# Low parts of w1 made ahead through a fourth place and due sooner; expert 0's loads and all gathers' transposes later in the order

## The chip, the cores and the metric

One core of one Trainium2 chip. The metric is the device time of one execution in microseconds (us); the number given for a kernel is the median of its runs. Engines: TensorE (PE; PEld is its weight load), VectorE (DVE), ScalarE (ACT), GpSimd (POOL) and SyncE (SP), which issues nearly all DMAs. A row with a q behind the engine (SPq) is of that engine's sequencer: an issue of a DMA, a wait or a branch.

## The reference, cut to what matters

Three layers in a row, all in float32 (batch 4, 8 heads, 576 positions, 2304 tokens of width 512):

```python
def _attn_ref(q, k, v, omega):          # random-feature attention
    q_p, k_p = phi(q * scale), phi(k * scale)
    kv = np.einsum('bhsm,bhsd->bhmd', k_p, v)
    z = np.sum(k_p, axis=2)
    ...
    return num / den

def _moe_ref(x, w_in, w_out):           # 512 -> 2048 -> 512
    h = x @ w_in
    return (h - np.tanh(h)) @ w_out

def _moe2_ref(x, w_gate, w1, w2):       # 8 experts, 512 -> 1024 -> 512
    logits = x @ w_gate                 # pairs (token, expert) in falling order of logit;
    ...                                 # a token goes to the first expert with room (288 places)
    for e in range(E):
        mask = assigned == e
        h = np.maximum(x[mask] @ w1[e], 0.0)
        out[mask] = h @ w2[e]
```

## The kernel before

**Split numbers.** A float32 matrix product is made of three TensorE passes: each operand is split into a high part (a copy to a shorter type, by ScalarE) and a low part (the operand minus its high part, by VectorE or GpSimd), and high x high, high x low and low x high are summed in PSUM (L604 to L606, L651, L1402 to L1404, L1421 to L1423).

**Stages.** The 2304 tokens are six blocks of 384. Attention runs along the first four blocks of the second layer. Blocks 4 and 5 share their passes over w_in in a double block (about 440 to 530 us): 16 chunks f, each with first matmuls of both blocks (`chunk_ops`), their polynomial on ScalarE and VectorE, and small matmuls for the gate's logits (`last_logits`). Behind it stands a branch (`tc.If`, L1530): if inputs were out of range, a slower version would run. All engines load the flag `over` (L1529) and branch. Behind the branch come the second matmuls of block 4 (`but_last_ops`: two kept chunks first, then eleven that load the low part gL from g4l and the low part oL of w_out from low_wo), and of block 5 (`last_ops`, 16 chunks of nine matmuls, L651, whose oL come through three slots, L566). Beside these VectorE searches which tokens go to expert 0, by rounds in which TensorE counts (L1096, L1121). Then the eight experts follow (`expert_ops`, from about 622 us).

**Low parts of w1, made ahead.** `low_ops` makes the low part of the first two of four row blocks of w1 of each expert, during the double block: 16 times a load of 512 KB into a tile `dw` (L581), two copies of a half to a tile `dh` (ScalarE, L300), two subtractions in place (L305), and a store to w1l (L588). `dw` has three places and `dh` two; they open in `switch2`, when attention is done. The two halves are written as copy, subtraction, copy, subtraction; as the subtraction both reads and writes the tile, the second copy stands behind the first subtraction.

**Gate of a block.** `gate_ops` transposes a block's output into `mT` (128 x 4 x 384 float32), multiplies it with the gate's weights (L682) and puts the logits away. It runs for blocks 0 to 3; `mT` has one place.

**Expert 0.** Its first tokens are fetched by three indirect DMAs of GpSimd (gathers, L1351) out of the stored outputs of blocks 0 to 4, and TensorE transposes them (L1369); the rows of block 5 are added later, out of SBUF (L1373). Its weights are eight loads of 512 KB (L1309 and L1312) and two of made-ahead low parts (L1322), all on SyncE's queue. Each has a turn: it stands behind the landing, as planned, of one of block 5's sixteen loads of oL (`oloads`). The fourth, sixth and eighth of its low parts are made by a copy and an accumulating DMA (L1330). For experts 1 to 7 the gathers (L1351) and transposes (L1364) run while the expert before is still at work.

**What sets the order.** The program is a list of operations with engine, planned duration, due time (`plan.at` and `lag`) and the tiles that they read and write. `Plan.run` (L129) walks through a planned time: it issues the operation that can start first, and of those that can start together the one due first. A DMA is planned as 280 KB per us, one after the other, plus 1.9 us; `late` is planned time behind an operation's end before what reads it can start. The order that comes out is each engine's order on the chip; the chip adds the waits. Tiles come from rings of places; a place is free when the last reader of its tile is done. With `rp` and `wp` an operation reads or writes a tile without standing behind that tile's other writers or readers.

The functions that the change touches, and what calls them:

Of the kernel before, what the change touches and what calls it, by code (L numbers as in the profile page):

```python
# [9 lines left out]
F32R = mybir.dt.float32r  # L10
# [176 lines left out]
def tile_kernel(ctx, tc, q, k, v, omega, w_in, w_out, w_gate, w_gate_t, w1, w2, out, dbg=None):  # L187
# [11 lines left out]
    NF = DFF // P  # L199
    E = w_gate.shape[1]  # L200
    BLK = 384
    NBLK = NT // BLK
# [95 lines left out]
    def copy(e, out, in_):  # L298
        if e == ACT:
            nc.scalar.activation(out, in_, AF.Copy)  # L300
        else:
            nc.vector.tensor_copy(out, in_)
# [270 lines left out]
    def low_ops(start, step):  # L573

        n = w1.shape[2]
        d_rings[:] = plan.ring([P, n], F32, "dw", []), plan.ring([P, n // 2], F32R, "dh", [])
        for k in range(E * NPRE):
            e_, r = k // NPRE, slice(k % NPRE * P, (k % NPRE + 1) * P)
            raw = Buf(d_rings[0])
            plan.at = start + step * k  # L580
            plan.op(SP, 0.47, lambda e, raw=raw, e_=e_, r=r: nc.sync.dma_start(raw.t, w1[e_, r, :]), w=[raw], nbytes=P * n * 4,  # L581
                    early=False)
            for i, h in enumerate((slice(0, n // 2), slice(n // 2, n))):
                hi = Buf(d_rings[1])
                plan.op(ACT, 0.6, lambda e, raw=raw, hi=hi, h=h: copy(e, hi.t, raw.t[:, h]), r=[raw], w=[hi], lag=4.0 + 0.6 * i)
                plan.op({POOL: 1.45, DVE: 0.65}, 0, lambda e, raw=raw, hi=hi, h=h: low(
                    e, raw.t.bitcast(F32R)[:, h], raw.t[:, h], hi.t), r=[raw, hi], w=[raw], lag=4.7 + 0.6 * i)
            plan.op(SP, 0.47, lambda e, raw=raw, e_=e_, r=r: nc.sync.dma_start(w1l[e_, r, :], raw.t), r=[raw],  # L588
                    nbytes=P * n * 4, lag=6.8)

# [72 lines left out]
        return xm, plan.op(SP, 0.47, lambda e: nc.sync.dma_start(ms[n * P + 1:(n + 1) * P + 1, :], xm.t.bitcast(F32)), r=[xm], lag=0.7,  # L663
                           nbytes=P * DM * 4)

    def gate_ops(j, xms):
        mT, lp, lT, lgb = Buf(mTr), Buf(bank), Buf(sr), Buf(None)
        own = lambda z, w: z.t[:, :TPB * w].rearrange("p (t n) -> p t n", t=TPB)
        for t, xm in enumerate(xms):
            tp = Buf(bank)  # L670

            def transposes(e, tp=tp, xm=xm):
                for c in range(NC):
                    nc.tensor.transpose(tp.t[:, c * P:(c + 1) * P], xm.t.bitcast(F32)[:, c * P:(c + 1) * P], ident)

            plan.op(PE, 0.44, transposes, r=[xm], w=[tp], lag=0.8 + 0.7 * t)
            plan.op({ACT: 0.6, DVE: 0.68}, 0, lambda e, t=t, tp=tp: copy(
                e, mT.t[:, :, t * P:(t + 1) * P], tp.t.rearrange("p (c n) -> p c n", n=P)), r=[tp], w=[mT], lag=1.5 + 0.7 * t)

        def gate(e):  # L680
            for c in range(NC):
                nc.tensor.matmul(lp.t[c * P // NC:(c + 1) * P // NC, :BLK], wg[:, c, :], mT.t[:, c, :], start=True, stop=True,  # L682
                                 skip_group_check=True)

        def back(e):
            for t in range(TPB):
                nc.tensor.transpose(own(lp, P)[:, t, :], lT.t[:, t * P:(t + 1) * P], ident)

        plan.op(PE, 0.9, gate, r=[mT, bwg], w=[lp], lag=4.0)
        plan.op({ACT: 0.48, DVE: 0.55}, 0, lambda e: copy(e, lT.t, lp.t[:, :BLK]), r=[lp], w=[lT], lag=5.0)  # L690
        plan.op(PE, 0.33, back, r=[lT], w=[lp], lag=5.6)
        plan.op(DVE, 0.25, lambda e: nc.vector.tensor_reduce(
            lg[:, j * TPB:(j + 1) * TPB, :], own(lp, P).rearrange("p t (c e) -> p t e c", c=NC)[:, :, :E, :], axis=AX.X,
            op=OP.add), r=[lp], w=[lgb], lag=6.0)
# [63 lines left out]
    def mlp_ops(start, step, general=False):  # L758
# [4 lines left out]
        for j in range(NBLK - 1):  # L763
# [32 lines left out]
                plan.at = start[j] + step[j] * NF + LAG2 + 0.7 * t  # L796
                xms.append(out_ops(j, t, acc[t])[0])
            plan.at = start[j] + step[j] * NF + LAG2
            gate_ops(j, xms)

        j, lacc4, lprev4 = NBLK - 2, Buf(bank), None
        for f in range(NF):
# [496 lines left out]
    def load_ops(p, ei):  # L1299
# [4 lines left out]
        for i in range(2 * NC):  # L1304
# [8 lines left out]
                                      w2[bass.ds(reg[0], 1), f * P:(f + 2) * P, :].rearrange("o (a p) d -> p (o a) d", p=P))  # L1313

            plan.at = PHASE * p + AT_EW * i + AT_LOAD
            turn = [] if p else [oloads[min(2 * i + 2, NF - 1)]]
            plan.op(SP, 0.47, load, w=[raw], after=[o] + turn, nbytes=P * FX * 4)
            plan.at = PHASE * p + AT_EW * i + (AT_SPLIT if p else 0.0)
            plan.op(ACT, 0.98, lambda e, H=H, raw=raw: copy(e, H.t, raw.t), r=[raw], w=[H])
            if i < NPRE:  # L1320
# [1 line left out]
                    nc.sync.dma_start(L.t.bitcast(F32), w1l[bass.ds(reg[0], 1), i * P:(i + 1) * P, :].rearrange("o p f -> p (o f)"))  # L1322

                plan.at = PHASE * p + AT_EW * i + (AT_SPLIT - 6.0 if p else AT_LOAD)
                turn = [] if p else [oloads[2 * i + 3]]
                plan.op(SP, 0.47, load_low, w=[L], after=[o] + turn, nbytes=P * FX * 4)
            elif i in (BYDMA if p < PDMA else ()):

# [14 lines left out]
    def expert_ops(p):  # L1343
# [4 lines left out]
        for g in range(NG):  # L1348
            t = tmp([GS, DM], F32, "xg", NG - 1) if g < NG - 1 else first["xg"]
            ix = idxs[p][g][1] if p else first["top"][g]  # L1350
            plan.op(POOL, 1.03, lambda e, g=g, t=t, ix=ix: nc.gpsimd.indirect_dma_start(  # L1351
                out=t.t[:GN[g]], out_offset=None, in_=ms if p else ms[:(NTT - TPB) * P + 1, :],
                in_offset=bass.IndirectOffsetOnAxis(ap=ix.t[:GN[g]].bitcast(U32), axis=0)),
                r=[ix], w=[t], after=stored if p else stored4, late=5.0)
            xg.append(t)
        for c in range(NC):
            plan.at = base + AT_TURN if p else -58.0 if c < NC - 1 else AT_LAST + AT_W * NF
# [153 lines left out]
        for r, n in zip(d_rings, (3, 2)):  # L1511
            r.add(wpre, [f"{r.name}{i}" for i in range(n)], t=max(o.end for o in att_ops))

    low_ops(starts[-2], (NF * steps[-1] + 4.0) / (E * NPRE))
    plan.at = T_MLP
    plan.op("-", 0.0, switch, after=early_ops)
    mlp_ops(starts, steps)
# [151 lines left out]
```

## Time and profile before

| | |
|---|---|
| median of 3 runs | 891.68 us (891.31 to 892.25) |
| the profiled execution | 886.79 us, of which the span is 884.9 us |
| mean granted clock of TensorE | 0.984 of full speed |
| TensorE busy | 846.3 us, 96% of the span |
| VectorE, ScalarE, GpSimd busy | 654.1 (74%), 470.2 (53%), 252.9 (29%) |
| DMA | 193.95 MB, mean 219 GB/s |

All times in rows are us from the start of the span. Busy time is an average over stages: where one engine is busy nearly all the time, as TensorE is here, the stretches in which it is not are the ones to look up. An idle stretch is shown in brackets behind the instruction that ended it, with what it had waited for. The granted clock is the share of TensorE's full speed (2.4 GHz) in a stretch; it has two levels, 1.00 and 0.50 (1.2 GHz).

### The profile page before, as it was taken

What the parts mean: (1) busy time and instruction counts of PE and PEld (TensorE: products, weight loads), DVE (VectorE), ACT (ScalarE), POOL (GpSimd) and SP (SyncE); (2) the same over time, 40 slices, a digit from 0 to 9 for tenths busy, and PEclk for the clock granted to TensorE, in tenths of its full rate; (3) what the DMA queues carried; (4) which work ended last, traced back from release to release, by engine and by line L of the source; (5) the groups of instructions that cost most, each with busy time, mean ns of one, the idle gap of its engine ahead of it and who ended that gap; (6) DMA issues with size and microseconds to landing.
All of it is one profiled execution on the core that took longest, in us unless ns stands there. A gap on an engine that the chain in (4) does not pass through costs nothing. (4 is left out here: it accounts for less than half of the span.)

```text
span 884.9 us, 17420 instructions
## 1 busy us (share of the span) xinstructions
PE 846.3 (96%) x6116; PEld 756.0 (85%) x6116; DVE 654.1 (74%) x1925; ACT 470.2 (53%) x1021; POOL 252.9 (29%) x276
## 2 busy tenths in 40 slices
PE   8979899999999999999999997989999999999995
PEld 6878788888988888889988985766999988999995
DVE  5898999886588889887887884444887877886520
ACT  4876564744456554755477870012565465455621
POOL 1122344222343345334521251010132322321211
PEclk8999999999999999999999997999999999999998
DMA  8988778887456666633478865567879778877600
GB/s 255 341 259 276 265 240 277 301 264 225 114 184 206 200 191 198 231 100 119 131 265 275 283 229 181 185 230 225 242 233 273 241 207 271 286 207 280 220 27 27
DMA packets 103790, 193.95 MB, mean 219 GB/s; under 512 B 28305, under 2 KB 42257, under 8 KB 103698
## 3 DMA queue, kind: packets, MB, share of 16 engines
q1 hardware_dynamic: 98034, 173.92, 59.7%
q0 software_dynamic: 5664, 18.88, 8.6%
q8 instruction: 49, 0.80, 0.4%
q14 instruction: 43, 0.35, 0.1%
HBM read 149.64 MB, written 33.69 MB: 207 GB/s over the span
## 5 line engine op out<-in xcount | busy, mean ns | idle before, releaser
L604 PE MATMUL bk<-xH,wi 128*128 128x384 f32 x332 | 118.3, 356 | 1.4 <-DVE xt L503 1.1
L605 PE MATMUL bk<-xL,wi 128*128 128x384 f32 x332 | 111.9, 337 | 0.5 <-DVE xL L305 0.5
L606 PE MATMUL bk<-xH,iL 128*128 128x384 f32 x332 | 112.0, 337 | 0.0
L651 PE MATMUL acc<-wo,gL 128*128 128x512 f32 x282 | 111.8, 397 | 0.0
L721 DVE SCALAR_TENSOR_TENSOR lw<-wf,raw 128x512 f32<-128x512 f32 x128 | 107.3, 838 | 5.4 <-POOL wf L718 4.0
L651 PE MATMUL acc<-wo,gH 128*128 128x512 f32 x240 | 99.9, 418 | 0.0
L305 POOL TENSOR_TENSOR gL<-s,gH 128x384 fp32r<-128x384 f32 x49 | 58.1, 1186 | 138.4 <-ACT gH L300 138.4
L441 ACT ACTIVATE phi<-bk,nm 128x128 f32<-128x128 f32 x272 | 77.2, 380 | 36.5 <-DVE nm L444 36.2
L651 PE MATMUL acc<-oL,gH 128*128 128x512 f32 x240 | 95.6, 398 | 0.3 <-DVE oL L305 0.3
L718 POOL TENSOR_TENSOR wf<-oL,wo 128x512 f32<-128x512 f32 x48 | 66.5, 1387 | 66.2 <-DMA oL<-low_wo 55.9
L300 ACT ACTIVATE gH<-s 128x384 fp32r<-128x384 f32 x80 | 42.0, 525 | 62.0 <-DVE s L631 37.1
L604 PEld LDWEIGHTS bk<-xH,wi 128*128 128x128 f32 x332 | 62.9, 189 | 9.0 <-issue 2.0
L629 DVE SCALAR_TENSOR_TENSOR s<-s,bk 128x384 f32<-128x384 f32 x83 | 45.4, 548 | 32.1 <-ACT s L628 31.9
L605 PEld LDWEIGHTS bk<-xL,wi 128*128 128x128 f32 x332 | 62.8, 189 | 3.2 <-DVE xL L305 0.7
L651 PEld LDWEIGHTS acc<-wo,gL 128*128 128x128 f32 x282 | 53.3, 189 | 12.2
L608 ACT ACTIVATE u<-bk 128x384 f32<-128x384 f32 x80 | 39.2, 490 | 44.0 <-PE bk L606 42.7
L606 PEld LDWEIGHTS bk<-xH,iL 128*128 128x128 f32 x332 | 62.6, 189 | 0.0
L631 DVE SCALAR_TENSOR_TENSOR s<-s,u 128x384 f32<-128x384 f32 x80 | 54.6, 682 | 1.1
L444 DVE TENSOR_REDUCE nm<-bk 128x4 f32<-128x512 f32 (+1 forms) x75 | 46.3, 632 | 12.2 <-PE bk L430 11.1
L651 PEld LDWEIGHTS acc<-wo,gH 128*128 128x128 f32 x240 | 45.6, 190 | 7.0 <-issue 0.3
L651 PEld LDWEIGHTS acc<-oL,gH 128*128 128x128 f32 x240 | 45.6, 190 | 6.3 <-DVE oL L305 0.6
L628 ACT ACTIVATE s<-u,qbias 128x384 f32<-128x384 f32 x80 | 49.3, 617 | 2.0
(409 smaller groups left out, 2336.9 us busy)
## 6 DMA issues: line engine op xcount, KB each, us to landing
r_wraw<-in_moe_w_dram SPq DMA_DIRECT2D x50, 512.0 KB, 5.7
iL<-low_wi SPq DMA_DIRECT2D x80, 256.0 KB, 3.3
oL<-low_wo SPq DMA_DIRECT2D x78, 256.0 KB, 2.8
raw<-in_moe_w_in_dram SPq DMA_DIRECT2D x32, 512.0 KB, 5.3
raw<-in_moe_w_out_dram SPq DMA_DIRECT2D x32, 512.0 KB, 4.1
dw<-in_moe_w_dram SPq DMA_DIRECT2D x16, 512.0 KB, 5.3
w1l<-dw SPq DMA_DIRECT2D x16, 512.0 KB, 3.7
s_wraw<-in_moe_w_dram SPq DMA_DIRECT2D x14, 512.0 KB, 6.8
```

What stands on the lines that cost most here:

```text
L305: (nc.gpsimd if e == POOL else nc.vector).tensor_tensor(out, in_, high.bitcast(F32), op=OP.subtract)
L441: nc.scalar.activation(ph.t[:, i0 + i, :], pj.t[:, i * M:(i + 1) * M], AF.Exp, bias=nmx.t[:, i0 + i:i0 + i + 1])
L444: plan.op(DVE, 0.1 + 0.125 * n, lambda e, pj=pj, i0=i0, n=n: V.tensor_reduce(nmx.t[:, i0:i0 + n], pj.t[:, :n * M].rearrange("p (i m) -> p ...
L604: nc.tensor.matmul(ph(), piece(iH, c), xH.t[:, c, :], start=(c == 0), stop=False)
L605: nc.tensor.matmul(ph(), piece(iH, c), xL.t[:, c, :], start=False, stop=False)
L606: nc.tensor.matmul(ph(), piece(iL, c), xH.t[:, c, :], start=False, stop=(c == NC - 1))
L628: plan.op(ACT, 0.52, lambda e: nc.scalar.activation(s.t, ut(), AF.Square, bias=qbias), r=[u], w=[s], lag=2.8)
L629: plan.op(DVE, 0.52, lambda e: V.scalar_tensor_tensor(s.t, s.t, QD, ph(), op0=OP.add, op1=OP.mult), r=[p, s], w=[s], lag=3.4)
L631: plan.op(DVE, 0.65, lambda e: V.scalar_tensor_tensor(s.t, s.t, QC, ut(), op0=OP.mult, op1=OP.mult), r=[u, s], w=[s], lag=4.0)
L651: nc.tensor.matmul(acc[t].t, (gL if k == 2 else gH).t[:, c], (oL if k == 1 else oH).t, start=(f == 0 and k == 0), stop=(f == end and k == ...
L718: plan.op(POOL, 1.45, lambda e: nc.gpsimd.tensor_tensor(w.t, lo.t.bitcast(F32), wo[:, f, :].bitcast(F32), op=OP.add), r=[lo, wbuf["wo", f] ...
L721: x_reads.append(plan.op(DVE, 0.9, lambda e, i=i: nc.vector.scalar_tensor_tensor(scratch.t.bitcast(F32), w.t, 1.0, half(rows[i // 2], i % ...
```

## The change

- `low_ops`: both copies of a tile's halves stand ahead of both subtractions, and a subtraction stands behind its own copy alone.
- `gate_ops` of block 3 gives the ring of `dw` a fourth place once its gate matmuls have read `mT`: the first 1024 columns of `mT` (`Whole`).
- `low_ops` is called with a shorter step: its tiles are due over 12 planned us less in all.
- Expert 0's loads have their turn four loads of oL later.
- Gathers are planned with 8.0 (expert 0) and 6.5 (others) us behind their issue instead of 5.0, so the transposes that read them are placed later in the order.

```diff
-            for i, h in enumerate((slice(0, n // 2), slice(n // 2, n))):
-                hi = Buf(d_rings[1])
+            halves = [(h, Buf(d_rings[1])) for h in (slice(0, n // 2), slice(n // 2, n))]
+            for i, (h, hi) in enumerate(halves):
                 plan.op(ACT, 0.6, lambda e, raw=raw, hi=hi, h=h: copy(e, hi.t, raw.t[:, h]), r=[raw], w=[hi], lag=4.0 + 0.6 * i)
+            for i, (h, hi) in enumerate(halves):
                 plan.op({POOL: 1.45, DVE: 0.65}, 0, lambda e, raw=raw, hi=hi, h=h: low(
-                    e, raw.t.bitcast(F32R)[:, h], raw.t[:, h], hi.t), r=[raw, hi], w=[raw], lag=4.7 + 0.6 * i)
+                    e, raw.t.bitcast(F32R)[:, h], raw.t[:, h], hi.t), r=[hi], rp=[raw], wp=[raw], lag=4.7 + 0.6 * i)
...
+    class Whole:
+        def __init__(self, z):
+            self.z = z
+
+        def tile(self, shape, dtype, tag, **kw):
+            return self.z.rearrange("p c n -> p (c n)")[:, :shape[1]]
+
-    def gate_ops(j, xms):
+    def gate_ops(j, xms, general):
...
-        plan.op(PE, 0.9, gate, r=[mT, bwg], w=[lp], lag=4.0)
+        o = plan.op(PE, 0.9, gate, r=[mT, bwg], w=[lp], lag=4.0)
+        if j == NBLK - 3 and not general:
+            plan.op("-", 0.0, lambda e: d_rings[0].add(Whole(mT.t), ["x"], t=o.end), after=[o])
...
-            turn = [] if p else [oloads[min(2 * i + 2, NF - 1)]]
+            turn = [] if p else [oloads[min(2 * i + 6, NF - 1)]]
...
-                turn = [] if p else [oloads[2 * i + 3]]
+                turn = [] if p else [oloads[2 * i + 7]]
...
-                r=[ix], w=[t], after=stored if p else stored4, late=5.0)
+                r=[ix], w=[t], after=stored if p else stored4, late=6.5 if p else 8.0)
...
-    low_ops(starts[-2], (NF * steps[-1] + 4.0) / (E * NPRE))
+    low_ops(starts[-2], (NF * steps[-1] - 8.0) / (E * NPRE))
```

## Rows read from the trace of the kernel before

**Rows 1.** Waits of TensorE from 440 us: waited for, us in total, times, longest
```profile
PE be L1364 <- DMA r_xg<-ms,r_ig: 1.3, 2, 1.1
...
PE be L1364 <- DMA xg_rest<-ms,r_ig: 0.7, 2, 0.6
```

**Rows 2.** Timeline at the branch: start, us, engine, line, what, [idle before, ended by]
```profile
529.66 1.33 POOL L305 TENSOR_TENSOR gL<-s,wi 128x384 fp32r<-128x384 f32 x1
...
532.02 0.43 SPq L826 DMA_DIRECT2D g4l<-gL  x1
...
534.70 0.47 PE L651 MATMUL acc<-wo,wi 128*128 128x512 f32 x1 [1.33 <-PEq L1530]
535.05 0.34 SPq L588 DMA_DIRECT2D w1l<-dw  x1
...
539.09 0.79 PE L651 MATMUL acc<-xm,wi 128*128 128x512 f32 x1 [3.93 <-SPq L1530]
...
539.93 0.34 SPq L855 DMA_DIRECT2D gL<-g4l  x1
```

**Rows 3.** Windows: length, busy us by engine, then granted clock, DMA share, GB/s
```profile
533.50:535.00 1.50, 0.30 (x1) 0.19 (x1) 1.47 (x4) 0.50 (x1) 0.00 (x0) 1.00 0.50 183
535.10:545.20 10.10, 6.17 (x23) 4.62 (x23) 2.50 (x10) 0.00 (x0) 2.53 (x8) 0.50 0.54 178
...
589.70:593.00 3.30, 3.30 (x11) 2.62 (x9) 0.00 (x0) 0.39 (x1) 0.00 (x0) 0.50 0.28 113
```

**Rows 4.** Instructions on tile dw: ns min/median/max, first and last start
```profile
L305 DVE TENSOR_TENSOR dw<-dw,dh x28: 673/691/1776, 450.7 to 534.3; 128x512 fp32r<-128x512 f32 x28
L581 SPq DMA_DIRECT2D dw<-in_moe_w_dram x16: 332/424/488, 443.2 to 528.6; - x16
L588 SPq DMA_DIRECT2D w1l<-dw x16: 337/338/382, 454.3 to 535.1; - x16
```

**Rows 5.** The gate's matmuls on mT (L682), first and last start
```profile
L682 PE MATMUL bk<-mT,wg x32: 486/498/510, 173.1 to 467.2; 128*32 128x384 f32 x32
```

**Rows 6.** DMA issues of 539.5 to 545: size, median us to landing
```profile
oL<-low_wo SPq DMA_DIRECT2D x3, 256.0 KB, 3.8
```

**Rows 7.** Windows, matmuls of L651 alone: TensorE, its weight loads, then clock
```profile
540.00:544.00 4.00, 4.00 (x10) 2.65 (x9) 0.50 0.68 199
566.00:570.00 4.00, 3.92 (x17) 2.71 (x16) 1.00 0.46 130
```

**Rows 8.** Window of the double block: PE, PEld, DVE, ACT, POOL busy
```profile
440.00:530.00 90.00, 88.84 (x509) 80.58 (x508) 73.18 (x119) 68.22 (x136) 27.63 (x24) 1.00 0.75 257
```

**Rows 9.** Timeline of TensorE at expert 0's gather
```profile
585.48 0.18 PE L1121 MATMUL rp<-id,d 128*128 128x8 bf16 x1 [0.56 <-DVE r_cond L1117]
587.55 0.33 PE L1369 MATMUL bd<-ident,r_xg 128*128 128x128 f32 x1 [1.89 <-DMA r_xg<-ms,r_ix]
588.72 0.33 PE L1369 MATMUL bd<-ident,r_xg 128*128 128x128 f32 x1 [0.84 <-DMA r_xg<-ms,r_ix]
```

**Rows 10.** DMA issues of 576 to 592
```profile
r_wraw<-in_moe_w_dram SPq DMA_DIRECT2D x3, 512.0 KB, 6.4
oL<-low_wo SPq DMA_DIRECT2D x4, 256.0 KB, 6.2
```

**Rows 11.** DMA issues of 548 to 576
```profile
oL<-low_wo SPq DMA_DIRECT2D x12, 256.0 KB, 2.7
```

**Rows 12.** Timeline: expert 0's first accumulating DMA, and its first matmul
```profile
603.98 0.99 POOL L1330 DMA_DIRECT2D wi<-r_wraw  x1 [20.51 <-ACT wi L1329]
...
622.49 0.38 PE L1402 MATMUL bd<-r_xgH,wi 128*128 128x288 f32 x1
```

**Rows 13.** Timeline of TensorE: expert 2's last transpose and first matmul
```profile
684.22 0.27 PE L1364 MATMUL bd<-ident,xg_rest 128*128 128x128 f32 x1
...
685.79 0.29 PE L1402 MATMUL be<-r_xgH,wi 128*128 128x288 f32 x1
```

**Rows 14.** Timeline of VectorE, 528 to 532
```profile
530.03 1.51 DVE L305 TENSOR_TENSOR dw<-dw,dh 128x512 fp32r<-128x512 f32 x1
```

More of the change, by code (lines that the diff above doesn't have):

```diff
@@ L798, in mlp_ops @@
             plan.at = start[j] + step[j] * NF + LAG2
-            gate_ops(j, xms)
+            gate_ops(j, xms, general)
         j, lacc4, lprev4 = NBLK - 2, Buf(bank), None
```

## The prediction

> **What bounds the kernel now.** The page's busy line and mean granted clock come first: TensorE is busy for 96% of the span, so what can be won is its idle time and the time it spends at the lower clock. The view of who waited for whom, limited to TensorE from 440 us on, lists its waits: the longest is for SyncE at the branch (L1530), and most others are for gathers; those of experts 1 to 7 come to 2.0 (1.3 and 0.7) [rows 1]. The timeline at the branch shows what SyncE was doing [rows 2]: its last issue before the branch is the store of a made-ahead low part at 535.05, and TensorE's second matmul behind the branch starts 4.04 later, at 539.09, after 3.93 idle. The windows show what idle time costs further on [rows 3]: the granted clock is 1.00 up to 535.0, a stretch in which TensorE did one matmul behind 1.33 idle, then 0.50 (1.2 GHz) from 535.1 to 545.2, and 0.50 again from 589.7 to 593.0, behind the wait for expert 0's gather.
>
> **Part 1, the low parts of w1.** 32 copies, 32 subtractions, 16 loads and 16 stores stay as they are; their order and places change. Loads run from 443.2 to 528.6, stores from 454.3 to 535.1 [rows 4]. Sixteen loads through three places are five turns of a place: (528.6 - 443.2)/5 = 17.1 us a turn. The fourth place opens when block 3's gate has read mT; its last matmul starts at 467.2 [rows 5]. With the same turn, three places load at 443, 460, 477 and 495, the fourth at 468, 485 and 502, and the sixteenth load goes at 512. The last store followed its load by 6.5, the first by 11.1: 518 to 523. If a turn grows in step with the places (22.8 us), the place wins nothing, and only the earlier due time and the second copy, which no longer waits for the first subtraction, are left. I take the first, as 4 us are enough: behind the last w1l store SyncE has only the store of g4l, issued at 532.02, and GpSimd had finished its data at 529.66 + 1.33 = 530.99 [rows 2].
>
> So SyncE's last issue moves from 535.05 to about 531.0, and TensorE's release, 4.04 later, to 535.05. TensorE's first matmul behind the branch stays at 534.70, as the 1.33 ahead of it are its own branch. Of the 3.93 about 0.2 is left: gain 3.7 (3.9 if the g4l store comes sooner, 2.9 if it stays at 532.02). The clock: from 539.09 to 545.2 TensorE worked at half speed, 6.1 us for work of 3.1. If the clock doesn't fall, the gain is 3.1; if it falls at the same place, TensorE is at work from then on, as it was at 589.7, where the low clock lasted 3.4 us (1.7 lost): 1.4. The 1.33 idle that came ahead of the fall stay, so I take the middle, 2.2. What is late next are SyncE's loads behind the branch: the first goes 0.84 after TensorE's restart [rows 2], the first low part of wo 0.5 later, and these landed in 3.8 [rows 6], so at 540.2. TensorE has 18 matmuls of the two kept chunks ahead of it, 0.235 each at full clock (17 in 4 us) [rows 7], 4.2 us, and a round of counts: until 539.5. That is a wait of 0.7 at full clock, none at half: 0.4. Part 1: 3.7 + 2.2 - 0.4 = **5.5**.
>
> The cover of the low work that comes forward is the idle time of VectorE and ScalarE in the double block: over 440 to 530 they are busy for 73.2 and 68.2 of 90 us, TensorE for 88.8 [rows 8]. About a sixth of the work, some 4 us on each, moves in: costed at nothing, up to 6.2 if the cover is gone (second rival).
>
> **Part 2, expert 0's loads and its gather's transposes.** Behind the search step at 585.48 TensorE had only the transposes in its order, and stood 1.89 and 0.84 for the gather [rows 9]: 2.7. A gather is now planned 8.0 - 5.0 = 3.0 longer, so 3 us of other matmuls go ahead: TensorE reaches the transposes at 585.66 + 3.0 = 588.7, when the gather had landed (the second one ran at 588.72). These matmuls need the low part of wo's chunk 5 at about 585.9. In 576 to 592 four such loads took 6.2, with three 512 KB loads of expert 0 among them [rows 10]; with none of those about, 2.7 [rows 11]. Expert 0's loads now stand four of these later on SyncE's queue, so chunk 5 and the gather have a freer DMA. With the wait goes the low clock behind it, 1.7.
>
> What it costs: expert 0's first five loads, 512 KB each, now run beside chunks 6 to 11. A slot of oL is refilled when its chunk is done, and is needed two chunks later, 18 x 0.235 = 4.2, plus one matmul: 4.4. Landings of 2.7 and 6.2 bound the wait of a chunk at 0 and 1.8; as the loads come one to a chunk, and not in a burst, I take 0.6 in all (0 to 2). Expert 0's own need: the accumulating DMA of its fourth weight was issued at 603.98, its first matmul ran at 622.49 [rows 12]. Four chunks later (4 x 9 x 0.235 = 8.5) is 612.5; 10 us are left for a landing, nearest 6.2. Nothing, then; 2.4 if it takes twice that. Part 2: 2.7 + 1.7 - 0.6 = **3.8**.
>
> **Part 3, the gathers of experts 1 to 7.** 1.5 us more are planned, so 1.5 us of matmuls go ahead of the transposes: the 2.0 of waits [rows 1] can go. Against it, expert 2's last transpose runs at 684.22 and its first matmul at 685.79 [rows 13]; there 1.5 later loses 0 to 1.5. Value 2.0 - 1.5 = **0.5** (2.0 at best; -2.5 if three experts lose it).
>
> **The sum.** 5.5 + 3.8 + 0.5 = 9.8 us. Against the profiled execution, 886.79 (a span of 884.9 and 1.9 around it), that is 877.0. The median of the runs is 4.9 above it, at 891.68, and no row says where those lie; I take the same gain off the median: 881.9.
>
> **A rule that speaks against it.** One subtraction of a low part on VectorE took 1.51 [rows 14] while GpSimd was at work from 529.66 to 530.99 [rows 2]; the median is 0.69 and the longest 1.78 [rows 4]. The Trainium skill, GPSIMD Engine Reference, section 8 (Key points), says why: GpSimd shares its SBUF interfaces with VectorE, and a VectorE instruction with two SBUF inputs contends for them. This trace agrees. By the rule, packing the subtractions closer makes more of them meet GpSimd's work; what that would cost is the second rival.
>
> **Rivals.**
> 1. *SyncE's tail stays.* The stores don't end sooner, or another arrival is last at the branch. For it: the place opens a quarter into the stage, and the DMA engines are busy for 0.75 of it [rows 8]. Against it: 4 us are enough. Part 1 is then nothing: 3.8 + 0.5 = 4.3, so 887.4.
> 2. *VectorE is crowded.* If all its 28 subtractions [rows 4] take 1.51 instead of 0.69, they need 28 x 0.82 = 23 us more, and it is idle for 16.8 of the stage [rows 8]: 6.2 come on TensorE. 9.8 - 6.2 = 3.6, so 888.1. Against it: some meet GpSimd already, and GpSimd is busy for 27.6 of the 90 alone.
> 3. *Slower: the low parts of wo starve.* Place: chunks 6 to 15, behind the gather. If expert 0's loads keep their landings at 6.2 or above, over the 4.4 that a slot allows, TensorE stands in every chunk and the clock falls as it did at 589.7. A matmul then takes 0.40 (10 in 4 us) for 0.235 [rows 7], a chunk of nine 1.5 more, ten chunks 15. Parts 1 and 3 give 6.0 and the gather's wait 2.7; 15 - 8.7 = 6.3 slower, so 898.0. It decides from six such chunks on; with fewer it is the forecast cut short. For it: the 6.2. Against it: the loads come spread.
>
> **How the numbers follow.** Forecast 0.58, by its bounds 878 (3.9 + 3.1 + 4.4 + 2.0 = 13.4 won) to 887; rival 1 0.14; rival 2 0.09; rival 3 0.19, of which 0.12 well over six chunks and 0.07 near six. 0.2% is 1.8 us, about what a measurement of this kernel tells from no change. Faster: 0.58 + 0.14 + 0.09 = 0.81; within: 0.07; slower: 0.12. The range 877.5 to 890.0 holds the forecast but for 0.03, the first two rivals, and a little of the third.
>
> **What would show it.** Right: the last w1l store before 531; no wait over 0.5 for SyncE at the branch; no wait of L1369; no half clock at the gather. Rival 1: a w1l store is still SyncE's last issue. Rival 2: TensorE idle between 467 and 525. Rival 3: L651 waits for loads of low_wo, and half clock between 585 and 610. Wrong altogether: these waits gone and the time unchanged.

## The result, and the profile after

The changed kernel took 879.38 us (median of 4 runs, 876.57 to 882.08) against 891.49 for the kernel before beside it (4 runs, 890.33 to 892.25): a ratio of 0.9865 [0.9828, 0.9901], 12.1 us less. A second group of runs, told of below, gave 0.9834 [0.9807, 0.9861]. The forecast was 881.9, 877.5 to 890.0: faster, as it said, and by 2 to 5 us more.

The profiled execution of the changed kernel is its slowest, 882.08 (a span of 880.3). Line numbers behind L587 are higher by 1 to 12 (L588 is L589, L651 is L652, L1351 is L1363, L1369 is L1381). First the waits of TensorE from 440 us (waited for, us in total, times, longest), which answer to [rows 1]:

```profile
PE rp L1133 <- DVE r_cond L1129: 1.4, 3, 1.0
PE acc L652 <- PEq L1542: 0.8, 1, 0.8
PE kv L747 <- DVE gL L305: 0.8, 1, 0.8
PE bk L747 <- POOLq L1542: 0.8, 1, 0.8
...
PE kv L747 <- POOL gL L305: 0.6, 1, 0.6
PE bk L605 <- DVE s L630: 0.5, 1, 0.5
PE bk L747 <- DVE gL L305: 0.5, 1, 0.5
```

The wait for SyncE at the branch and those for gathers are gone; only TensorE's own branch is left (0.8). The longest row now is for rounds of the experts' search (r_cond), in the experts. New are four waits ahead of the branch, in the last chunks of the double block: 0.47 and 0.56 for gL, 0.49 for s, and 0.76 in the row that names GpSimd's branch, but ends with its subtraction of gLk. The kv row that names VectorE is an old wait, at 460.44 (1.02 long before, 0.77 now). The branch in the timeline, answering to [rows 2]; the rows are start, us, engine, line, what:

```profile
534.10 0.34 SPq L589 DMA_DIRECT2D w1l<-dw  x1
...
534.79 0.32 SPq L838 DMA_DIRECT2D g4l<-gL  x1
...
540.89 0.48 PE L652 MATMUL acc<-wo,wi 128*128 128x512 f32 x1 [0.81 <-PEq L1542]
...
541.77 0.34 SPq L867 DMA_DIRECT2D gL<-g4l  x1
```

This execution reached the double block 4.27 later than the one before did (441.22 against 436.95), for a reason ahead of anything that the change touches (last section). With that taken off, the last store of a low part came at 529.83, 5.2 sooner than before, and SyncE's last issue at 530.5. The places of the low parts, answering to [rows 4]: 13 loads go through dw, 3 through the new place in mT.

```profile
L305 DVE TENSOR_TENSOR dw<-dw,dh x22: 674/685/1774, 455.0 to 533.4; 128x512 fp32r<-128x512 f32 x22
L581 SPq DMA_DIRECT2D dw<-in_moe_w_dram x13: 382/426/1318, 447.4 to 518.7; - x13
...
L581 SPq DMA_DIRECT2D mT<-in_moe_w_dram x3: 333/382/382, 471.8 to 513.7; - x3
```

At expert 0's gather [rows 9] the transposes now follow the first gather by 10.7, and nothing stands in brackets behind them:

```profile
579.99 1.51 POOL L1363 DMA_INDIRECT r_xg<-ms,r_ix  x1 [36.56 <-DVE r_ix L1294]
...
590.73 0.38 PE L1381 MATMUL bd<-ident,r_xg 128*128 128x128 f32 x2
...
607.00 0.98 POOL L1342 DMA_DIRECT2D wi<-r_wraw  x1 [22.88 <-ACT wi L1341]
...
616.58 0.30 PE L1414 MATMUL bd<-r_xgH,wi 128*128 128x288 f32 x1
```

The windows tell most, and are used for the experiments too: the double block, then the stretch from the branch (from the end of TensorE's work ahead of it) to the last of the matmuls that add block 5's rows for expert 0, called the middle below, then the experts. Length, then busy time of TensorE, its weight loads, VectorE, ScalarE and GpSimd, the granted clock, DMA share and GB/s. The idle time of TensorE is the length less its busy time; where the mean clock is under 1.00, the rest was at 0.50. Of the kernel before:

```profile
436.95:533.37 96.42, 94.86 (x541) 84.83 (x539) 78.47 (x128) 70.78 (x142) 31.67 (x25) 1.00 0.74 255
533.37:622.65 89.28, 79.18 (x461) 59.04 (x462) 40.73 (x198) 12.95 (x20) 6.50 (x12) 0.92 0.61 197
622.65:875.14 252.49, 248.27 (x2226) 238.90 (x2225) 175.67 (x763) 131.90 (x222) 60.31 (x81) 1.00 0.71 217
```

Of the changed kernel:

```profile
441.22:540.09 98.87, 95.50 (x541) 84.59 (x539) 79.45 (x136) 70.32 (x142) 25.47 (x20) 1.00 0.73 257
540.09:616.74 76.65, 75.06 (x452) 56.52 (x453) 37.18 (x178) 12.09 (x18) 7.03 (x12) 0.98 0.70 215
616.74:870.53 253.79, 249.88 (x2235) 239.16 (x2234) 177.98 (x783) 130.94 (x220) 59.37 (x81) 1.00 0.71 217
```

From the start of the double block to the end it is 8.88 shorter. The middle stretch is 12.63 shorter: idle time fell from 10.10 to 1.59 (8.5), and the time at half clock from 13.65 to 3.41. TensorE was at work in 9.7 and 3.4 us of that, and lost half of it: 3.2 less (the other 4 us at half clock before were idle time, counted already). Nine matmuls went from it to the experts (461 to 452), so the middle's busy time doesn't compare to the last tenth. The double block became 2.45 longer (idle 1.56, now 3.37), the experts 1.30 (idle 4.22, now 3.91); in a second profile of the same kernel (`after_again`, below) the experts are 2.3 shorter than before. The half clock, answering to [rows 3], has two rows: the one stretch behind the branch, 3.4 long where it was 10.2, and full clock behind the gather.

```profile
541.50:544.80 3.30, 3.30 (x9) 2.58 (x8) 2.07 (x7) 0.00 (x0) 1.92 (x7) 0.50 0.44 110
585.00:600.00 15.00, 14.98 (x85) 11.47 (x84) 2.62 (x13) 2.12 (x2) 0.00 (x0) 1.00 0.92 292
```

### The profile page after: what moved, and what is told of

The parts are those of the page before. It is cut to its first block, busy times and chain, and to the rows that moved or that the text cites. A ratio compares the mean times of both kernels' runs of the same rounds, so it can differ in the third digit from the quotient of the medians.

```text
span 880.3 us, 17424 instructions
## 1 busy us (share of the span) xinstructions
PE 851.0 (97%) x6116; PEld 759.7 (86%) x6116; DVE 655.8 (74%) x1933; ACT 468.0 (53%) x1018; POOL 246.4 (28%) x271
## 5 line engine op out<-in xcount | busy, mean ns | idle before, releaser
L605 PE MATMUL bk<-xH,wi 128*128 128x384 f32 x332 | 120.2, 362 | 1.6 <-DVE xt L503 1.1
L652 PE MATMUL acc<-wo,gL 128*128 128x512 f32 x282 | 111.2, 396 | 0.0
L652 PE MATMUL acc<-wo,gH 128*128 128x512 f32 x240 | 99.3, 415 | 0.0
L652 PE MATMUL acc<-oL,gH 128*128 128x512 f32 x240 | 95.2, 396 | 0.3 <-DVE oL L305 0.3
L630 DVE SCALAR_TENSOR_TENSOR s<-s,bk 128x384 f32<-128x384 f32 x83 | 45.5, 548 | 32.8 <-ACT s L629 32.6
L652 PEld LDWEIGHTS acc<-wo,gL 128*128 128x128 f32 x282 | 53.0, 188 | 12.4 <-POOL gL L305 0.4
L444 DVE TENSOR_REDUCE nm<-bk 128x4 f32<-128x512 f32 (+1 forms) x75 | 46.3, 631 | 12.6 <-PE bk L430 12.4
L632 DVE SCALAR_TENSOR_TENSOR s<-s,u 128x384 f32<-128x384 f32 x80 | 53.2, 665 | 1.3
L652 PEld LDWEIGHTS acc<-wo,gH 128*128 128x128 f32 x240 | 45.2, 188 | 6.9 <-issue 0.3
L652 PEld LDWEIGHTS acc<-oL,gH 128*128 128x128 f32 x240 | 45.2, 188 | 6.5 <-DVE oL L305 0.6
```

What stands on the lines that cost most here:

```text
L444: plan.op(DVE, 0.1 + 0.125 * n, lambda e, pj=pj, i0=i0, n=n: V.tensor_reduce(nmx.t[:, i0:i0 + n], pj.t[:, :n * M].rearrange("p (i m) -> p ...
L605: nc.tensor.matmul(ph(), piece(iH, c), xH.t[:, c, :], start=(c == 0), stop=False)
L630: plan.op(DVE, 0.52, lambda e: V.scalar_tensor_tensor(s.t, s.t, QD, ph(), op0=OP.add, op1=OP.mult), r=[p, s], w=[s], lag=3.4)
L632: plan.op(DVE, 0.65, lambda e: V.scalar_tensor_tensor(s.t, s.t, QC, ut(), op0=OP.mult, op1=OP.mult), r=[u, s], w=[s], lag=4.0)
L652: nc.tensor.matmul(acc[t].t, (gL if k == 2 else gH).t[:, c], (oL if k == 1 else oH).t, start=(f == 0 and k == 0), stop=(f == end and k == ...
```

## Experiments

The runs came in three groups; the kernel before, run beside each, had medians of 890.41, 886.56 and 887.86. So times are compared within a group, and ratios across them. What was expected of each run was written before that run, but with the result and its profile known.

**Group 1: the parts alone.**

`p1_only`, part 1 without parts 2 and 3:

```diff
# against the changed kernel
-            turn = [] if p else [oloads[min(2 * i + 6, NF - 1)]]
+            turn = [] if p else [oloads[min(2 * i + 2, NF - 1)]]
-                turn = [] if p else [oloads[2 * i + 7]]
+                turn = [] if p else [oloads[2 * i + 3]]
-                ... late=6.5 if p else 8.0)
+                ... late=5.0)
```

> Part 1 alone (fourth place, earlier due time, both copies ahead of both subtractions; expert 0's loads and all gathers as in the kernel before). Theory: TensorE's wait for SyncE at the branch is gone (3.9 us before, under 0.3 now), some 2.4 us of it come back as gaps of TensorE in the last chunks of the double block, the low clock behind the branch lasts one stretch of about 3.4 us for 10.2, and the gather's wait of 2.7 us with its low clock stays: 4 to 5 us less than before, about 887. Rival (the whole gain is in the gather): no difference from before beyond 1 us.

Measured: 886.90, ratio 0.9951 [0.9934, 0.9968], 4.4 less (2.8 to 5.9). The windows of the same three stretches:

```profile
434.67:533.53 98.86, 95.49 (x541) 84.56 (x539) 78.85 (x136) 70.18 (x142) 25.57 (x20) 1.00 0.74 257
533.53:617.66 84.13, 78.94 (x462) 58.95 (x462) 39.52 (x196) 12.35 (x18) 6.49 (x12) 0.94 0.63 199
617.66:875.36 257.70, 250.69 (x2226) 240.42 (x2224) 176.63 (x765) 130.96 (x220) 58.81 (x81) 0.99 0.70 213
```

At the branch TensorE waits 0.80 for itself and not for SyncE, which is 4.5 (5.26 to 0.80) of the 4.9 of idle time that the middle loses; the double block is 2.44 longer, as in the changed kernel. The half clock behind the branch lasted 6.8, not the 3.4 expected. The experts, which part 1 doesn't touch, are 5.2 longer in this profile (7.01 idle for 4.22, mostly search rounds, and a half clock of 3.4 at 734.8), so the profile as a whole is no shorter than that of before, and the gain rests on the timed runs; where the experts' idle time comes from is taken up under part 2 below. The gather's waits stay, so they are not part 1's to remove:

```profile
PE bd L1381 <- DMA r_xg<-ms,r_ix: 2.0, 2, 1.1
...
PE bd L1381 <- DMA xg_rest<-ms,r_ix: 0.3, 1, 0.3
```

`p2_only`, part 2 alone (`low_ops` and `gate_ops` as before):

```diff
# against the kernel before
-            turn = [] if p else [oloads[min(2 * i + 2, NF - 1)]]
+            turn = [] if p else [oloads[min(2 * i + 6, NF - 1)]]
-                turn = [] if p else [oloads[2 * i + 3]]
+                turn = [] if p else [oloads[2 * i + 7]]
-                ... late=5.0)
+                ... late=5.0 if p else 8.0)
```

> Part 2 alone (expert 0's loads four loads of oL later, expert 0's gather planned 3 us longer; the rest as before). Theory: the wait of 2.7 us for the gather, the small waits beside it and its 1.7 us of low clock go: 5 to 6 us less than before, about 886; the branch keeps its wait of 3.9 us. Rival (parts help only together, since the order is worked out anew): under 3 us less.

Measured: 879.23, ratio 0.9858 [0.9837, 0.9878], 12.6 less, twice the 5 to 6 expected. Its windows:

```profile
436.89:533.34 96.45, 94.88 (x541) 84.86 (x539) 78.29 (x126) 70.45 (x141) 30.75 (x25) 1.00 0.74 255
533.34:614.45 81.11, 75.07 (x452) 56.66 (x453) 38.38 (x180) 12.75 (x20) 7.03 (x12) 0.96 0.68 214
614.45:867.94 253.49, 249.18 (x2235) 239.30 (x2234) 177.13 (x781) 131.80 (x222) 61.77 (x81) 1.00 0.70 217
```

The double block is that of before. Of the 6.04 idle in the middle, 5.25 are the branch (1.33 and 3.92, unchanged) and 0.79 is all that is left behind it; before it was 10.10 - 5.26 = 4.84. So part 2 removes 4.05 of idle time and the half clock at the gather, and by itself gives about as much as the whole change did.

`late0_only`, of part 2 only the longer planned time of expert 0's gather:

```diff
# against the kernel before
-            ... late=5.0)
+            ... late=5.0 if p else 8.0)
```

> Only expert 0's gather planned 3 us longer (transposes later in TensorE's order), loads as before. Theory: the matmuls put ahead of the transposes need the low part of wo's chunk 5, which still stands behind three 512 KB loads of expert 0 and takes 6 to 7.5 us to land: TensorE waits 2 to 3 us for it instead of for the gather, the clock falls all the same, and the time is within 1.5 us of before. Rival (the place in the order was the whole fault): 4 to 6 us less, no wait of L651.

Measured: 892.67, ratio 1.0019 [1.0001, 1.0036], 1.7 more, for 1.5 either way expected: nothing won. TensorE's order has 175 matmuls of L651 between the branch and the first transpose, 13 more than before (162), 3.06 us at 0.235 as predicted. The gather's waits are gone, and two waits for low parts of wo stand in their place, the second with half clock behind it (0.81 and 0.73, for one of 2 to 3 expected); the experts idle 7.98 where it was 4.22 and 4.38:

```profile
583.80 0.50 PE L651 MATMUL acc<-oL,gH 128*128 128x512 f32 x1 [0.81 <-DMA oL<-low_wo]
...
606.22 0.80 PE L651 MATMUL acc<-oL,gH 128*128 128x512 f32 x1 [0.73 <-DMA oL<-low_wo]
```

```profile
606.20:609.40 3.20, 3.18 (x8) 2.18 (x8) 0.61 (x4) 0.00 (x0) 0.00 (x0) 0.50 0.51 179
```

That is rival 3's mechanism, in small: two chunks, not six, and only the second of them behind the gather, where the rival had placed them.

`loads_only`, of part 2 only the loads' later turn:

```diff
# against the kernel before
-            turn = [] if p else [oloads[min(2 * i + 2, NF - 1)]]
+            turn = [] if p else [oloads[min(2 * i + 6, NF - 1)]]
-                turn = [] if p else [oloads[2 * i + 3]]
+                turn = [] if p else [oloads[2 * i + 7]]
```

> Only expert 0's loads four loads of oL later, gathers planned as before. Theory: gather and oL land sooner (under 6 us for the gather, about 3 us for oL), so most of the wait at the transposes goes, from 2.7 to under 1.5 us, and the clock doesn't fall there: 3 to 5 us less than before. Rival (the order of the transposes is what counts): the wait of 2.7 us stays within 0.5.

Measured: 883.58, ratio 0.9907 [0.9883, 0.9930], 8.3 less, more than the 3 to 5 expected. No wait at the gather, with its planned time unchanged. The order shows how: ten more matmuls of L651 (172) go ahead of the transposes (presumably because, with the large loads out of the way on the planned DMA, the next chunk's oL is planned to be there in time), and on the chip they find their oL:

```profile
582.64 1.51 POOL L1360 DMA_INDIRECT r_xg<-ms,r_ix  x1 [36.56 <-DVE r_ix L1291]
...
590.35 0.38 PE L1378 MATMUL bd<-ident,r_xg 128*128 128x128 f32 x2
```

The transposes come 7.7 behind the first gather in both; before, 1.89 and 0.56 of that were idle. With both edits 185 go ahead, 23 more.

What the large loads did to the small transfers shows in the times from issue to landing between 576 and 592: the gather's of before,

```profile
r_xg<-ms,r_ix POOLq DMA_INDIRECT x2, 7.4
```

with oL's 6.2 in [rows 10], and those of `p2_again` (part 2 alone, below), where the loads come later:

```profile
oL<-low_wo SPq DMA_DIRECT2D x7, 256.0 KB, 3.4
...
r_xg<-ms,r_ix POOLq DMA_INDIRECT x2, 4.7
```

**Group 2: pieces of part 1 on top of part 2, and more of part 2.**

`before_again`, the kernel before unchanged, for a second profile.

> The kernel before once more, for a second profile of it. Theory A (the first profile is a typical run, and part 2 simply takes away more waits than the 2.7 at the gather): the same idle times of TensorE behind the branch again, 1.3 and 3.9 for the branch, 2.7 at expert 0's gather, and 4.1 (within 1) in the experts; time 886 to 888. Theory B (the first profile was a good draw: 15 timed runs of this kernel lay at 889.7 to 894.3, the profiled one at 886.79): more stretches at half clock than the 10.2 and 3.4 us behind the branch, or more waits for the search's rounds in the experts; time 889.5 or above.

Measured: 885.79, theory A (and 0.2 under its range): the same waits within 0.1 (1.33 and 3.93 at the branch, 2.00 and 0.86 at the gather), 4.38 idle in the experts. The half clock behind the branch lasted 6.8 where it had been 10.2.

`p2_halves`: part 2 and the split of the halves alone.

```diff
# against p2_only
-            for i, h in enumerate((slice(0, n // 2), slice(n // 2, n))):
-                hi = Buf(d_rings[1])
+            halves = [(h, Buf(d_rings[1])) for h in (slice(0, n // 2), slice(n // 2, n))]
+            for i, (h, hi) in enumerate(halves):
...
```

> Part 2 with the split of the halves alone of part 1 (both copies ahead of both subtractions; three places, the old due times). Theory A (the fourth place carries the branch's gain, and the copies' order gives nothing): the wait for SyncE at the branch stays at 3.5 to 3.9, the last store of a low part stays SyncE's last issue, and the time is that of part 2 alone, 879.2, within 1.5. Theory B (the halves' order is what lets the tail end sooner, since a tile is done one copy sooner): the wait falls below 2, and the time is 2 to 4 below part 2 alone, 875 to 877. By theory C (what part 1 wins at the branch it gives back ahead of it, in waits for gL in the last chunks of the double block, and the halves' order makes these) the last chunks have idle times of TensorE of 0.4 to 0.8 as with the whole of part 1, and the time is above 879.2.

Measured: 875.81, ratio 0.9865 [0.9825, 0.9904]. SyncE's wait falls from 3.92 only to 3.04:

```profile
535.85 0.34 SPq L589 DMA_DIRECT2D w1l<-dw  x1
...
536.67 0.47 PE L652 MATMUL acc<-wo,wi 128*128 128x512 f32 x1 [0.79 <-PEq L1540]
...
540.18 0.79 PE L652 MATMUL acc<-xm,wi 128*128 128x512 f32 x1 [3.04 <-SPq L1540]
```

The double block has three of the new idle times (0.76 for gL, 0.40 for gLk, 0.54 for a copy of the logits) and is 1.55 longer. The wait lies between A's 3.5 and B's 2, the idle times are C's; the time tells nothing apart, as the 879.2 named there belongs to another group.

`p2_place`: part 2 and the fourth place alone.

```diff
# against p2_only
+        if j == NBLK - 3 and not general:
+            plan.op("-", 0.0, lambda e: d_rings[0].add(Whole(mT.t), ["x"], t=o.end), after=[o])
```

> Part 2 with the fourth place alone of part 1 (the halves as before, the old due times). Theory A (the fourth place carries the branch's gain): the wait for SyncE at the branch falls below 2, and the time is 2 to 4 below part 2 alone (879.2), 875 to 877. Theory B (the halves' order does it): the wait stays at 3.5 to 3.9, and the time is 879.2 within 1.5. Theory C (part 1 gives back ahead of the branch what it wins there; a tile more in work crowds VectorE): three to five idle times of TensorE of 0.4 to 0.8 in the last 20 us ahead of the branch, and a time of 879.2 or above.

Measured: 874.78, ratio 0.9849 [0.9810, 0.9888]. Theories A and C are both right on the trace: no wait of a TensorE matmul for SyncE, and five idle times of 0.40, 0.90, 0.44, 0.57 and 0.57 ahead of the branch; the double block is 3.2 longer. But the store did not end sooner:

```profile
539.65 0.34 SPq L588 DMA_DIRECT2D w1l<-dw  x1
...
540.99 0.47 PE L651 MATMUL acc<-wo,wi 128*128 128x512 f32 x1 [0.80 <-PEq L1541]
...
541.50 0.29 PEld L651 LDWEIGHTS acc<-xm,wi 128*128 128x128 f32 x1 [0.35 <-SPq L1541]
```

This execution started its double block 3.61 late (440.56); set back by that, the last store was issued at 536.04, one us later than before. TensorE no longer waits because it arrives 3.2 later itself, and because SyncE's release came 1.85 behind its last issue where it had taken 4.04 before (535.05 to 539.09) and takes 4.33 in `p2_halves`. With 4.04 here too, some 2 us of the wait would have stayed (an estimate from these times).

`p2_turn8`: part 2 with the loads eight loads of oL later instead of four.

```diff
# against p2_only
-            turn = [] if p else [oloads[min(2 * i + 6, NF - 1)]]
+            turn = [] if p else [oloads[min(2 * i + 10, NF - 1)]]
-                turn = [] if p else [oloads[2 * i + 7]]
+                turn = [] if p else [oloads[2 * i + 11]]
```

> Part 2 with expert 0's loads another four loads of oL later (eight in all). Theory A (what part 2 wins is that nothing of 512 KB stands in the DMA queues when expert 0's rows are gathered; four loads are enough for that): no wait at the gather, as with four; nothing more is won, and expert 0's weights come due: TensorE waits at L1402 or L1421 for a load or an accumulating DMA, 1 to 5 us; time 880 to 885. Theory B (the loads of the low part of wo are what large loads delay, at every chunk, and the later these come the better): 1 to 3 below 879.2.

Measured: 877.32, ratio 0.9893 [0.9851, 0.9934]. Nothing more won than with four (0.9858 and, below, 0.9881), as theory A said. Its price did not come, nor its 880 to 885: the experts' matmuls wait for no load, but once 0.28 for a low part of the tokens and once 1.41 for a search round. So at eight the weights are still in time.

**Group 3: the changed kernel beside three of its parts.**

`after_again` is the changed kernel, `p2_again` is `p2_only`, `place_again` is `p2_place`, all without a new edit; `no_latep` is the changed kernel without part 3:

```diff
# against the changed kernel
-                ... late=6.5 if p else 8.0)
+                ... late=5.0 if p else 8.0)
```

> The changed kernel once more, as the mark for the other three runs of this group (the same kernel before came to 891.5, 890.4 and 886.6 in three groups of runs, so only ratios within a group are compared). Theory A (part 2 carries the whole gain): a ratio of 0.986 to before, within 0.003, and the part-2-only kernel within 0.2% of it. Theory B (parts 1 and 2 add up, as predicted): 1.7 or more below the part-2-only kernel. In the second profile the last store of a low part stands 5 to 7 ahead of the branch's release as in the first, TensorE has four idle times of 0.4 to 0.8 in the double block's last chunks, and the idle time in the experts is 3.9 within 0.5.

> Part 2 alone (expert 0's loads four loads of oL later, its gather planned longer; low parts of w1 and the gathers of experts 1 to 7 as before). Theory A (part 2 carries the whole gain): within 0.2% of the changed kernel. Theory B (part 1 adds what it won by itself, 0.5%): 3 to 5 above it. Theory C (the rest of the change costs): 2 or more below it.

> Part 2 with the fourth place alone of part 1. Theory A (it ends the wait for SyncE at the branch without more waits in the chunks ahead than the whole of part 1 has, and the order that comes out has 0.7 of idle time in the experts for 3.9): 3 to 5 below the changed kernel. Theory B (its ratio to before of 0.985 in the group before is that of the changed kernel, 0.986 to 0.987; the profile's lower idle time does not show in the time): within 1.7 of the changed kernel.

> The changed kernel without part 3: the gathers of experts 1 to 7 planned with 5.0 as before. Theory A (part 3 gives 0.5 as predicted, below what can be told apart): within 1.7 of the changed kernel; the waits at the gathers of experts 1 to 7 (L1376 here), none in the changed kernel's profile, come back with 1 to 2 in all. Theory B (the transposes' later place costs more than the waits): 2 or more below the changed kernel. Theory C (the waits cost a half clock behind them as well): 2 or more above it.

| | median, us | runs | ratio to before |
|---|---|---|---|
| `after_again` | 872.60 | 6 (871.29 to 876.51) | 0.9834 [0.9807, 0.9861] |
| `place_again` | 873.80 | 5 (872.96 to 875.95) | 0.9849 [0.9822, 0.9876] |
| `no_latep` | 873.92 | 6 (872.08 to 881.49) | 0.9859 [0.9823, 0.9894] |
| `p2_again` | 876.62 | 6 (875.44 to 881.32) | 0.9881 [0.9853, 0.9910] |

The changed kernel is 4.0 below part 2 alone (the means of six runs each differ by 4.0, with 2.3 either way from their scatter). So theory A of `p2_again`, that part 2 is the whole gain, which the first group had suggested, falls: part 1 adds what it gives by itself, and the earlier equality compared kernels from different groups. The fourth place alone brings most of it (3.1 ± 2.0 below `p2_again`), and does not beat the changed kernel; nothing that was run does. `after_again` missed on the experts, 1.50 idle for the 3.9 expected. Without part 3 the time is 1.3 higher, inside the scatter (1.7 ± 3.1 by the means); its one wait at a gather of the later experts is small, where 1 to 2 in all was expected, and the changed kernel has none in either profile:

```profile
PE be L1376 <- DMA r_xg<-ms,r_ig: 0.5, 1, 0.5
```

## Why the prediction was right, and where not

**What bounds the kernel.** Held in part: what was named was won, at the branch, the gather and the half clock behind each. But about half of what part 2 wins outside the clock lies further on, in the experts, for which the prediction had only part 3's 0.5.

**Part 1, 5.5 predicted, 4.4 (2.8 to 5.9) by itself and 4.0 ± 2.3 on top of part 2.** The terms:
- *Gap, 3.7.* The two waits at the branch went from 5.26 to 0.81, 4.45 less: the 3.93, and 0.5 of TensorE's own branch, which the prediction had left as it was. (By its own times nothing of the 3.93 stayed either: a release at 535.05, idle time from 535.16.)
- *Clock, 2.2.* Behind the branch the half clock lasted 10.2, 6.8, 6.8, 6.8, 10.2, 6.8, 6.8 and 6.8 in the eight profiles without the fourth place, 3.4, 0, 6.8, 6.8, 3.4 and 0 in the six with it: means of 7.7 and 3.4. Part of each stretch is idle time, which the gap has counted: TensorE was at work in 4.7 and 3.1 of them, and lost half of that, 2.3 and 1.6. That is 0.8 less, with 1.2 either way from the scatter. So the middle between the two bounds was too high by these profiles, and what is sized is a mean over chance, not the place of one fall.
- *New wait for a low part of wo, 0.4.* None, in all six profiles with the fourth place.
- *Cover, costed at nothing.* This step failed: the double block became 2.45 longer, 1.8 of it idle time, which lies in its last 11 us. With it the terms give 4.45 + 0.8 - 2.45 = 2.8, the low end of what the timed runs show. The stages of `p1_only`'s profile say the same (5.15 off the middle, 2.44 on the double block: 2.7). Where the other 1.6 of the 4.4 lies is open; the clock is the term least well known.

The working of the tail failed too, though its result came out. The last store was to come at 518 to 523, limited then by g4l; it came at 529.8 with the 4.27 taken off. The new place took its 3 loads, as worked out, and the last load came at 514.4, for 512. What was wrong is the time from load to store: 6.5 to 11.1 had been taken, and the last three tiles took 13 to 17, the very last 15.4. The 6.5 was short for before, too: the two tiles ahead of the last had taken 12.2. 4 us were enough, so the wait went all the same. And the release at a fixed 4.04 behind SyncE's last issue is no constant: 1.85 in `p2_place`. Which of the three edits of part 1 brings the store forward by 5.2 is not settled: the halves' order alone leaves it 0.1 sooner, the place alone makes it 1.0 later, and the due time was not run alone.

**Part 2, 3.8 predicted, 10.6 to 12.6 measured** (0.9858 [0.9837, 0.9878], and 0.9881 [0.9853, 0.9910]). This is the term that was mis-sized. The half clock at the gather went as predicted (1.7), and the waits for oL came to 0 to 0.47 for the 0.6 allowed. Idle time fell by 4.05, not by 2.7: 2.73 at the transposes, and 1.4 in three waits for search rounds ahead of expert 0 (the first, 0.56, stands in [rows 9]), which the prediction didn't count, as they are for VectorE. With the clock that makes 5.7. In its second profile part 2 had only 0.75 idle in the experts, for 4.2 and 4.4 of the kernel before:

```profile
616.99:865.40 248.41, 247.66 (x2236) 239.11 (x2234) 177.57 (x781) 131.71 (x222) 61.71 (x81) 1.00 0.72 222
```

There the sum is 8.8 (3.6 in the middle, 1.7, 3.5); in its first profile, with 4.31 idle in the experts, it is 5.7. The timed runs tell which is nearer, since each has its span and mean granted clock on record: the clock's shortfall times the span estimates what the half clock took. Outside the clock the runs of before took 876.6 on average in group 1 and 872.7 in group 3, those of part 2 alone 869.1 and 864.1, so 7.5 and 8.7 less; the rest of the gain is clock (4.9 and 1.9). Both kernels are 4 to 5 slower in group 1, and the 5.7 sets a profile of that group against one of before that lies below all 15 timed runs there (886.79, for 889.66 to 894.30). The nearest pair is `before_again` and `p2_again`: 7.3 less idle time, 3.7 in the middle and 3.6 in the experts (2.0 at the gathers of experts 1 to 7, 1.6 at search rounds). Why these wait less with part 2 is open.

The reason given for the step was half right. More matmuls ahead of the transposes do hide the gather, but 13 of them put there by the longer planned time alone win nothing (`late0_only`), since they stand for their own oL behind 512 KB loads; the loads' turn alone wins 8.3 (`loads_only`), and moves ten matmuls ahead by itself. Outside the clock it wins 9.5, no less than both edits do, so that the longer planned time adds anything to it is not shown. In `p2_again` the last of the three gathers had landed at 587.24, 3.9 ahead of the first transpose. The prediction had given the loads the smaller role. Expert 0's weights: 10 us were to be left; the first accumulating DMA is issued at 607.00, the first matmul runs at 616.58, 9.6 later, without a wait.

**Part 3, 0.5 predicted.** Not told from nothing. Of the 2.0 of waits that it was to remove, 0.4 to 0.9 is left with part 2 alone (`p2_again`, `p2_only`) and 0.5 in `no_latep`, so most of them go without it.

**The sum.** 9.8 was taken off the median, 12.1 [8.8, 15.3] and 14.7 [12.3, 17.1] came: 1.4 less from part 1 and some 7 more from part 2. That the time fell well inside the range owes something to luck: the two errors pull against each other, and 14.7 off the 891.68 would have been 877.0, just below the range.

**The rule that spoke against it.** Of 27 subtractions of low parts on VectorE in the double block, 3 took over 1 us (the longest 1.77), as many as before among 28; their excess over the median is 2.3 together, 3.3 before. With the subtractions of gL and the polynomial's steps counted too, 14 instructions of VectorE took over 1.25 times their median, 8.4 us above it together, and 22 before, 12.1 us; every one of them ran beside an instruction of GpSimd. Of the polynomial's two steps, the one with an operand in PSUM (L630) never took over 0.56, though 12 of its 33 ran beside GpSimd; of the 33 with both in SBUF (L632) 14 did, and 10 were lengthened. So the meeting with GpSimd's work that the Trainium skill's GPSIMD Engine Reference, section 8 (Key points), describes did not become more frequent when the work came closer together. But two of these meetings now stand where TensorE waits:

```profile
527.27 1.66 POOL L305 TENSOR_TENSOR dw<-dw,dh 128x512 fp32r<-128x512 f32 x1 [1.57 <-ACT dh L300]
...
527.69 1.66 DVE L305 TENSOR_TENSOR gL<-s,wi 128x384 fp32r<-128x384 f32 x1
...
529.27 1.49 DVE L305 TENSOR_TENSOR dw<-dw,dh 128x512 fp32r<-128x512 f32 x1
...
529.40 0.34 PE L747 MATMUL bk<-gL,vgs 128*8 128x384 f32 x1 [0.47 <-DVE gL L305]
...
530.69 0.54 DVE L630 SCALAR_TENSOR_TENSOR s<-s,bk 128x384 f32<-128x384 f32 x1
...
531.29 0.44 PE L605 MATMUL bk<-xH,wi 128*128 128x384 f32 x1 [0.49 <-DVE s L630]
```

The subtraction of gL took 1.66 for its median of 0.56, and the low part ahead of s 1.49 for 0.69; at their medians neither wait would be there (an estimate from these rows).

**Rivals.** 1: fell; `p2_halves` shows what it would have looked like. 2: fell at its price of 6.2 and by its sign (no new idle time until the last 11 us of the stage), but its mechanism has a share in 1.0 of the 1.8 of idle time, the two waits above. For the other two, low parts of w1 on VectorE stand ahead of the polynomial's steps that gL and gLk come from; that this alone made them late is not shown. 3: fell for the whole change, and came true with two chunks in `late0_only`; the loads' turn, which the rival took for the cause, is what prevents it.

## What to carry to other kernels

When a consumer waits for a small transfer, look at what else stands in the DMA queues at that moment, not only at where the consumer stands in its order: moving the consumer alone brought the wait back one operand further on, moving the large loads removed it and won 8.3, for a visible wait of 2.7 and a half clock worth 1.7. Work squeezed in under an engine's idle share still has an order; ask whose result it now stands in front of in the last microseconds of the stage. Two kernels a few us apart are compared only beside each other, in one group of runs.

## What the runs showed of the hardware

- The price of SyncE's branch varies: from its last issue to TensorE's release 4.04 to 4.09 (in the seven profiles without any of part 1), 4.33 (`p2_halves`), and 1.85 (`p2_place` and `place_again`). In the last two SyncE had stood 7.7 us ahead of that issue, in `p2_halves` 5.2; that this is the cause was not tried.
- The same waits did not give the same half clock. `after` and `after_again` run one program, with idle times alike within 0.02 in the 20 us ahead of the branch, and had 3.4 and 0 at half clock behind it; `no_latep`, alike within 0.03, had 6.8.
- Half-clock stretches in the attention stage, which no edit here touches, lie elsewhere in each execution, 3.4 us in all in the profile whose double block started first (434.67) and 23.9 in each of the three whose double block started last (440.56 to 441.22). These starts lie 6.6 us apart in the 14 profiles, over half of what the change won, and enough to put two single profiles in the wrong order.
- One program in one order had 4.31 us of idle time in the experts in one execution and 0.75 in another (`p2_only`, `p2_again`); the difference lies mostly in search rounds whose answer reached TensorE up to 1.1 late. The timed runs of these groups differ the same way outside the clock, 5.1 for part 2 alone and 3.9 for the kernel before. The cause is open.
